# Windowed attention and a SiLU layer on one core: when the strided rows of batches 3 to 5 are loaded and transposed

## The chip, the core and the metric

The kernel runs on one core of a Trainium2 chip. A core has a matrix engine (TensorE, PE in the profile, with its weight loads shown apart as PEld), a vector engine (VectorE, DVE), a scalar engine (ScalarE, ACT), GpSimd (POOL) and SyncE (SP). Each engine has a queue of its own that runs in order; they meet through semaphores. POOL and SP here mostly start DMA transfers, which 16 DMA engines carry out. The metric is the device time of one run, in microseconds (us). Before the change it is 312.84 us, the median of three runs (312.16, 312.84 and 313.18).

## The reference

There are 8 batches, 8 heads, 576 positions and a head size of 64. Half of the heads look back over a window of 32 positions, the other half over every fourth position of the last 128. The attention's output goes through two dense layers with x * sigmoid(x) between them.

```python
scores = scale * np.matmul(q, k.transpose(0, 1, 3, 2))
mask_plain = (rel >= 0) & (rel < window)                                   # window = 32
mask_dil = (rel >= 0) & (rel < window * dilation) & (rel % dilation == 0)  # dilation = 4
masks = np.stack([mask_plain if h < H // 2 else mask_dil for h in range(H)], axis=0)
scores = np.where(masks[None], scores, -1e9)
attn = softmax(scores)                      # over the last axis
x = np.matmul(attn, v).transpose(0, 2, 1, 3).reshape(B * S, H * D)     # 4608 x 512
h = x @ w_in                                # 512 x 2048
out = ((h * sigmoid(h)) @ w_out)            # 2048 x 512, float32
```

## The kernel before

The dense layers are most of the work. For each batch `layer1` (L717) makes 16 blocks of 128 rows of h with 8 matmuls each, ScalarE applies the SiLU (L725), and `layer2` (L782) multiplies the result with w_out in tiles of 128 rows; VectorE copies a tile (L766) and SP stores it (L767) from one of five buffers, ob. One batch's two layers are a loop of steps, 0 to 47. Between them PE does the attention of the next batches in short groups.

The attention of a batch is split in two kinds, called z: z = 0 are the plain heads, z = 1 the strided heads, whose positions are regrouped by their remainder modulo 4. For each kind there are scores (L379 plain, L391 strided), exponentials on ScalarE (L560), a normalisation on VectorE (L576), a transpose of the probabilities and the product with v (L627, L691).

The scores need q and k with the head size on the partitions, so the rows that are loaded must be transposed. Up to batch 2 PE does this (L329). From batch 3 on it is done by DMA, in two steps:

- `load_rows(b)` runs on POOL. It loads q and k of batch b into one of two row buffers, nat (`natural[(b + 1) % 2]`). The plain rows are eight DMAs at L134, one for each head and each of k and q, with 128-byte pieces; the strided rows are four at L141, with 512-byte pieces. The argument zs sets which kind goes first.
- `cross(b, z)` runs on SP. For z = 0 it issues two transposing DMAs from nat to the buffer plain (L152, first k and then q), for z = 1 two to the buffer strided (L158, L159). plain and strided have two buffers each, for even and odd batches.

POOL also loads v (L177, L185, L190). SP also issues the stores and, from batch 3's strided heads on, the transposes of the probabilities pn (`turn_by_dma`, L600).

The order of all this is written out by hand. `plan_of(b)` holds, for the loop of batch b, lists of calls by step; `at(s, f, ...)` puts a call on step s, and calls of one step are issued in the order in which they were put there. In batch b's loop, steps 0 to 15 stand ahead of the 16 blocks of layer 1, and later steps ahead of each quarter of a tile of layer 2. No scheduler changes it: each engine's instructions stand in the order of these calls. An instruction waits on its own engine for what it reads, and for the readers of what it overwrites. So a DMA that SP issues waits at the head of SP's queue, and whatever stands behind it there waits as well. POOL's DMAs use eight semaphores in turn, so one waits until the eighth before it has landed.

What stands around the change, in the loops of batches 1 and 2:

- L852, in batch 0's loop: POOL loads the rows of batch 3, plain ones first.
- L870 to L872, in batch 1's loop: SP transposes batch 3's plain rows at step 2, its strided rows at step 20, and batch 4's plain rows at step 28.
- L878: POOL loads the rows of batch 4 at step 17, plain ones first.
- L893, in batch 2's loop: POOL loads the rows of batch 5 at step 0, plain ones first; later batches' rows are loaded strided ones first. They go into the buffer that held batch 3's.
- L895 and L896: at step 12, SP transposes the plain rows of batch b+3 and the strided rows of batch b+2.
- The strided scores of batch 3 are at step 11 of batch 2's loop, those of batch 4 at step 11 of batch 3's.

Of the kernel before, what the change touches and what calls it, by code (L numbers as in the profile page):

```python
# [29 lines left out]
def kernel(  # L30
# [764 lines left out]
    def transposes(at, b, z, step):  # L795
        for which in (1, 0):
            at(step, transpose, b, z, which, both)

    def later(at, b, z, steps, copies=(nc.vector.tensor_copy, nc.vector.tensor_copy)):

        for hi in (0, 1):
            if steps[hi] is not None:
                at(steps[hi], normal, b, z, hi)
        for hi in (0, 1):
            at(steps[2], turn, b, z, hi)
        for hi in (0, 1):
            at(steps[2], turned, b, z, hi, copies[hi])
        at(steps[3], values, b, z)
        at(steps[3], finish, b, z, copies)

    def plan_of(b):
        ev = {}

        def at(s, fn, *args):
            ev.setdefault(s, []).append((fn, args))

        def all_exps(b, z):
            for hi in (0, 1):
                at(16, exps, b, z, hi)

        if b == 0:

            at(-16, normal, 0, 1, 1)
            at(-15, shift_class, 0, dve, 1, 2)
            at(-14, normal, 0, 0, 1)
            at(-8, turn, 0, 1, 1)
            at(-8, turned, 0, 1, 1, act)
            at(-4, turn, 0, 0, 1)
            at(-4, turned, 0, 0, 1)
            at(-4, values0, 1, 1)  # L830
            at(-4, last_values, 0, 1, (1,))
            at(-4, finish0, 1, 1)
            at(-4, last_finish, 0, 1, 1)
            at(-2, values0, 0, 1)
            at(-2, last_values, 0, 0, (1,))
            at(-2, finish0, 0, 1, both)
            at(-2, last_finish, 0, 0, 1)
            at(-2, clear_short, 1, nc.vector)
            at(-2, load_v, 1)
            for c in (2, 3):  # L840
                at(-2, load_w_out, c)
            at(-2, load_qk, 2)
            transposes(at, 1, 1, 2)
            at(8, scores, 1, 1)
            for hi in (0, 1):
                at(8, shift, 1, 1, hi)
            for which in (1, 0):
                at(17, transpose, 1, 0, which, (dve, dve))
            at(20, normal, 1, 1, 0)
            at(20, scores, 1, 0)  # L850
            at(14, shift_v, 1, nc.sync.dma_start)
            at(17, load_rows, 3)  # L852
            at(17, load_v, 2)
            all_exps(1, 1)
            for hi in (0, 1):
                at(20, exps, 1, 0, hi)
            for n, z, hi in ((20, 1, 1), (26, 0, 0), (28, 0, 1)):
                at(n, normal, 1, z, hi)
            for n, z, copies in ((27, 1, (dve, dve)), (30, 0, both)):
                for hi in (0, 1):  # L860
                    at(n, turn, 1, z, hi)
                for hi in (0, 1):
                    at(n, turned, 1, z, hi, copies[hi])
                at(n + 1 + z, values, 1, z)
                at(n + 1 + z, finish, 1, z, both)
        elif b == 1:
            transposes(at, 2, 0, 2)
            transposes(at, 2, 1, 11)
            at(2, shift_v, 2, nc.sync.dma_start)
            at(2, cross, 3, 0)  # L870
            at(20, cross, 3, 1)
            at(28, cross, 4, 0)  # L872
            at(8, scores, 2, 0)
            for hi in (0, 1):
                at(8, shift, 2, 0, hi)
            at(17, nc.gpsimd.tensor_copy, latch, qTs[1][:, 1, S - 1 : S])
            at(17, load_v, 3)
            at(17, load_rows, 4)  # L878
            at(14, scores, 2, 1)
            all_exps(2, 0)  # L880
            all_exps(2, 1)
            for hi in (0, 1):
                at(19, normal, 2, 0, hi)
            at(21, scores, 3, 0)
            at(21, exps, 3, 0, 0)
            at(21, exps, 3, 0, 1)
            later(at, 2, 0, (None, None, 27, 28))
            later(at, 2, 1, (29, 31, 33, 34))
        else:
            if b + 2 < B:  # L890
                at(0, load_v, b + 2)
                if b + 3 < B:
                    at(0, load_rows, b + 3, (0, 1) if b == 2 else (1, 0))  # L893
                if b + 3 < B:
                    at(12, cross, b + 3, 0)  # L895
                at(12, cross, b + 2, 1)  # L896
            if b + 1 < B:
                at(1 if b == 2 else 0, shift_plain, b + 1, dve, 0, NM)
                at(12, shift_class, b + 1, dve, 0, 2)
                at(12, shift_over, b + 1, dve)  # L900
                if b == 2:
                    later(at, 3, 0, (0, 0, 4, 6))
                else:
                    at(6, values, b + 1, 0)
                    at(6, finish, b + 1, 0)
                at(11, scores, b + 1, 1)
                at(11, shift, b + 1, 1, 1)
                all_exps(b + 1, 1)
            if b + 2 < B:
                at(17, scores, b + 2, 0)  # L910
                for hi in (0, 1):
                    at(18, exps, b + 2, 0, hi)
            if b + 1 < B:
                for hi in (0, 1):
                    at(22 + hi, normal, b + 1, 1, hi)
                    at(22 + hi, turn_by_dma, b + 1, 1, hi)
                at(29, values, b + 1, 1)
                at(29, finish, b + 1, 1)
            if b + 2 < B:
                for hi in (0, 1):  # L920
                    at(27 + hi, normal, b + 2, 0, hi)
                    at(27 + hi, turn_by_dma, b + 2, 0, hi)

        def plan(s):
            for fn, args in ev.pop(s, ()):
                fn(*args)

        return plan
# [49 lines left out]
    for b in range(B):  # L978
        plan = plan_of(b)
        if b == 0:  # L980
            for x in range(NFF):
                plan(2 * x - NFF)
                plan(2 * x + 1 - NFF)
                layer1_part(2 * x % NFF, 2 * x // NFF, first[x] if x < 4 else None)
        else:
            for f in range(NFF):
                plan(f)
                layer1(b, f)
        if b == 0:
            layer2_first(plan)  # L990
        else:
            layer2(b, plan)
        for s in range(NFF, 3 * NFF):
            plan(s)
# [30 lines left out]
```

## Time and profile before

| | |
|---|---|
| median of three runs | 312.84 us (312.16 to 313.18) |
| the profiled execution, time | 313.66 us |
| the profiled execution, span | 311.9 us |
| PE busy | 298.2 us, 96% |
| VectorE busy | 180.1 us, 58% |
| ScalarE busy | 186.2 us, 60% |
| GpSimd busy | 91.5 us, 29% |
| DMA queue q0 (POOL's) | 18.88 MB |
| DMA queue q1 (SP's) | 19.60 MB |
| DMA queue q8 (instructions) | 35 transfers, 0.57 MB |

The span runs from the first to the last instruction; times in a timeline count from its start. In the groups and timelines a line has the engine, the line of the kernel, the operation, the tiles written and read, and how often; a bracket says how long the engine sat idle before it and what ended that, where "issue" means that the profile names nothing. SPq is SP's queue, in which issuing a DMA takes the time shown; the transfer itself goes on behind it. PEclk gives TensorE's granted clock in tenths for 40 equal slices of the span, 7.8 us each, and DMA how busy the DMA engines were.

The loops fall on these stretches: batch 1's from about 59 to 100 us, batch 2's from about 100 to 138 us, batch 3's from about 138 us on.

### The profile page before, as it was taken

How to read it: one execution, taken by the hardware profiler on the slowest of the kernel's cores; microseconds unless marked ns; L12 is line 12 of the kernel's file. 1: busy time of each engine (PE TensorE's matmuls, PEld its weight loads, DVE VectorE, ACT ScalarE, POOL GpSimd, SP SyncE). 2: the span in 40 equal slices, each digit the busy share in tenths (PEclk: the TensorE clock that was granted, in tenths of full speed). 3: DMA queues.
4: the chain of work that ended last, by engine and by line, in shares of the span. 5: the costliest groups of instructions: out<-in, count | busy, mean ns of one | idle time of the engine just before them, and what ended most of it. 6: DMA issues, size and time to landing. Idle time of an engine off the chain costs nothing.

```text
span 311.9 us, 10363 instructions
## 1 busy us (share of the span) xinstructions
PE 298.2 (96%) x4466; PEld 190.9 (61%) x4466; DVE 180.1 (58%) x372; ACT 186.2 (60%) x554; POOL 91.5 (29%) x139
## 2 busy tenths in 40 slices
PE   5889999999998979999999999999999999999995
PEld 2657755677455856467744676467744775468544
DVE  6896588627796725971687228871696245520011
ACT  1775658756992536955596357956694458336300
POOL 8535455920784442077104730040000000000000
PEclk9999999999999988999999999999999999999999
DMA  8999999997899999799967998399026100410021
GB/s 104 178 213 201 185 203 205 189 183 114 90 163 177 133 180 190 125 171 182 113 130 149 174 148 139 78 164 140 2 57 137 58 4 0 121 59 2 0 101 69
DMA packets 104878, 39.21 MB, mean 126 GB/s; under 512 B 79568, under 2 KB 100048, under 8 KB 104832
## 3 DMA queue, kind: packets, MB, share of 16 engines
q0 software_dynamic: 63104, 18.88, 60.0%
q1 hardware_dynamic: 41584, 19.60, 30.6%
q8 instruction: 35, 0.57, 0.8%
q14 instruction: 11, 0.09, 0.1%
q10 hardware_dynamic: 144, 0.07, 0.1%
HBM read 37.75 MB, written 9.44 MB: 151 GB/s over the span
## 4 chain that ended last, share of the span: by engine, by line
PE 82%; DMA 7%; DVE 5%; issue 3%; ACT 2%; POOL 1%; POOLq 0%; SPq 0%; ACTq 0%
PE h L717 36%; PE o L782 29%; PE o L756 5%; DMA w_in<-in_moe_w_in_dram 4%; PE h L737 4%; PE x L627 3%; DMA nat<-in_q_dram 2%; PE s L391 1%; PE s L379 1%; ACT pe L560 1%; DVE pn L576 1%; PE t L329 1%; DMA ptT<-pn 1%; DVE ms L512 1%; PE pt L585 1%
## 5 line engine op out<-in xcount | busy, mean ns | idle before, releaser
L725 ACT ACTIVATE gT<-h 128x576 f16<-128x576 f32 x112 | 72.9, 651 | 83.6 <-PE h L717 83.4
L717 PE MATMUL h<-xT,w_in 128*128 128x288 f16 x896 | 115.2, 289 | 0.0
L782 PE MATMUL o<-w_out,gT 128*128 128x512 f16 (+1 forms) x528 | 114.3, 373 | 0.1
L717 PEld LDWEIGHTS <-w_in 128*128 128x128 f16 x896 | 87.1, 99 | 24.3 <-DVE xT L704 0.3
L782 PEld LDWEIGHTS <-gT 128*128 128x128 f16 x528 | 50.6, 98 | 55.2 <-issue 0.3
L560 ACT ACTIVATE pe<-ms,nm 128x64 f32<-128x64 f32 x178 | 59.1, 334 | 4.2 <-DVE nm L528 4.2
L766 DVE COPY ob<-o 128x512 f32<-128x512 f32 (+1 forms) x34 | 23.1, 681 | 46.1 <-PE o L782 45.2
L512 DVE SCALAR_TENSOR_TENSOR ms<-s,mask 128x512 f32<-128x512 f32 x28 | 19.2, 686 | 40.3 <-PE s L391 27.5
L560 ACT ACTIVATION_READ_ACCUMULATOR pe<-ms,nm 128x1 f32 x178 | 33.5, 188 | 0.0
L704 DVE CAST xT<-x 128x512 f16<-128x512 f32 x26 | 16.8, 684 | 22.0 <-PE xs L691 22.0
L177 POOL DMA_DIRECT2D vw<-in_v_dram x16 | 10.0, 631 | 63.3 <-PE xs L691 57.3
L576 DVE TENSOR_TENSOR pn<-pe,r 128x640 f16<-128x640 f32 (+2 forms) x32 | 25.3, 792 | 1.1
L528 DVE TENSOR_REDUCE nm<-ms 128x10 f32<-128x640 f32 (+1 forms) x28 | 22.0, 787 | 1.0
L737 PE MATMUL h<-xT,w_in 128*128 128x256 f16 (+1 forms) x128 | 17.1, 286 | 1.8 <-issue 0.7
L134 POOL DMA_DIRECT2D nat<-in_q_dram x20 | 14.7, 757 | 8.0 <-DMA vw<-in_v_dram 4.3
L134 POOL DMA_DIRECT2D nat<-in_k_dram x20 | 15.1, 769 | 5.1 <-DMA nat<-in_q_dram 3.5
L737 PEld LDWEIGHTS <-w_in 128*128 128x128 f16 x128 | 12.0, 98 | 5.7 <-issue 1.8
L756 PE MATMUL o<-w_out,gT 128*128 128x512 f16 x64 | 15.0, 380 | 0.0
L744 ACT ACTIVATE gT<-h 128x512 f16<-128x512 f32 (+1 forms) x16 | 10.1, 651 | 6.5 <-PE h L737 6.3
L627 PEld LDWEIGHTS <-vw 64*64 64x64 f16 x896 | 8.6, 108 | 6.4 <-issue 6.2
L627 PE MATMUL x<-ptT,vw 64*64 64x32 f16 x896 | 10.4, 187 | 1.0 <-issue 0.9
L569 DVE TENSOR_REDUCE l<-pe 128x10 f32<-128x640 f32 (+2 forms) x12 | 9.6, 801 | 1.5 <-ACT pe L551 1.4
(101 smaller groups left out, 250.3 us busy)
## 6 DMA issues: line engine op xcount, KB each, us to landing
out_dram<-ob SPq DMA_DIRECT2D x35, 256.0 KB, 2.5
vw<-in_v_dram POOLq DMA_DIRECT2D x8, 288.0 KB, 6.6
vw<-in_v_dram POOLq DMA_DIRECT2D x16, 128.0 KB, 5.9
w_in<-in_moe_w_in_dram POOLq DMA_DIRECT2D x4, 512.0 KB, 12.6
w_out<-in_moe_w_out_dram POOLq DMA_DIRECT2D x4, 512.0 KB, 11.0
nat<-in_k_dram POOLq DMA_DIRECT2D x6, 256.0 KB, 7.1
nat<-in_q_dram POOLq DMA_DIRECT2D x6, 256.0 KB, 7.7
nat<-in_k_dram POOLq DMA_DIRECT2D x20, 72.0 KB, 6.8
```

The source lines that it names most:

```text
L134: nc.gpsimd.dma_start(out=f[:, 2 * (1 - which) + h // 2, 0 : ZR - 1, h % 2], in_=src[b, h].rearrange("(m p) d -> p m d", p=RT),)
L512: nc.vector.scalar_tensor_tensor(out=ms[:, 0:8].rearrange("p (n t) c -> p n (t c)", n=2), in0=s[hi].rearrange("p n t c -> p n (t c)"), sca ...
L528: nc.vector.tensor_reduce(out=nm[:, 0:w], in_=ms[:, 0:w], axis=AX.X, op=ALU.max, negate=True)
L560: nc.scalar.activation(pe[:, t, :], slot(t), AF.Exp, scale=1.0 if b else scale, bias=nm[:, t : t + 1], accum_out=l[:, t : t + 1],)
L576: nc.vector.tensor_tensor(pn[:, 0:w], a["pe", z, hi][:, 0:w], r[:, 0:w, None].broadcast_to([P, w, KB]), ALU.mult)
L627: nc.tensor.matmul(dst, w, p, start=True, stop=True)
L717: nc.tensor.matmul(h[:, half, 0:HS], w_in16[:, c, f * P : f * P + P], xT[:, c, half * HS : half * HS + HS], start=(c == 0), stop=(c == MC ...
L725: nc.scalar.activation(gT[:, f, s0 : s0 + S].rearrange("p (a c) -> p a c", a=2), h[:, :, 0:HS], AF.Silu)
L737: nc.tensor.matmul(h[:, i, 0 : c1 - c0], w_in16[:, c, (f + i) * P : (f + i + 1) * P], xT[:, c, c0:c1], start=(c == 0), stop=(c == MC - 1),)
L756: nc.tensor.matmul(o, gT[:, f, t * P : (t + 1) * P], w_out16[:, f, :], start=(f == 0), stop=(f == NFF - 1),)
L766: copy(ob, o)
L782: nc.tensor.matmul(o, gT[:, f, t * P : (t + 1) * P], w_out16[:, f, m0:m1], start=(f == 0), stop=(f == NFF - 1),)
```

## The change

Batch 3's strided transposes are issued at step 2 of batch 1's loop, right behind its plain ones, in place of step 20. Batch 4's strided transposes are issued at step 28 of batch 1's loop, right behind its plain ones, in place of step 12 of batch 2's loop, where they stood behind batch 5's plain transposes. From batch 5 on the strided transposes stay where they were. The rows of batch 5 are loaded strided ones first, as those of later batches are. No instruction is added or removed; PE, VectorE and ScalarE have the same order as before.

```diff
             transposes(at, 2, 1, 11)
             at(2, shift_v, 2, nc.sync.dma_start)
-            at(2, cross, 3, 0)
-            at(20, cross, 3, 1)
-            at(28, cross, 4, 0)
+            for z in (0, 1):
+                at(2, cross, 3, z)
+                at(28, cross, 4, z)
             at(8, scores, 2, 0)
...
                 if b + 3 < B:
-                    at(0, load_rows, b + 3, (0, 1) if b == 2 else (1, 0))
+                    at(0, load_rows, b + 3, (1, 0))
                 if b + 3 < B:
                     at(12, cross, b + 3, 0)
-                at(12, cross, b + 2, 1)
+                if b > 2:
+                    at(12, cross, b + 2, 1)
```

## The prediction

> **What bounds the kernel now.** Read first: the page's busy times and its slices. TensorE (PE) is busy 96% of 311.9 us, so only its idle time and its slow time can be won. Slices 15 and 16 (109 to 125 us) show a lowered clock, in the stretch where the DMA engines are busiest.
>
> ```profile
> span 311.9 us, 10363 instructions
> PE 298.2 (96%) x4466; PEld 190.9 (61%) x4466; DVE 180.1 (58%) x372; ACT 186.2 (60%) x554; POOL 91.5 (29%) x139
> ...
> PEclk9999999999999988999999999999999999999999
> DMA  8999999997899999799967998399026100410021
> ...
> q8 instruction: 35, 0.57, 0.8%
> ```
>
> Read second: the waits of PE. After the start-up (the first 25 us) three remain, and all end on "issue": nothing that the profile names.
>
> ```profile
> PE s L391 <- issue: 2.2, 1, 2.2
> PE x L627 <- issue: 0.9, 1, 0.9
> ...
> PE ss L391 <- issue: 0.3, 1, 0.3
> ```
>
> Read third: PE's timeline around the two long ones.
>
> ```profile
> 96.40 0.62 PE L627 MATMUL x<-ptT,vw 64*64 64x32 f16 x53
> 97.92 0.28 PE L627 MATMUL x<-ptT,vw 64*64 64x32 f16 x11 [0.90 <-issue]
> ...
> 107.14 5.07 PE L717 MATMUL h<-xT,w_in 128*128 128x288 f16 x40
> 112.15 0.58 PE L391 MATMUL s<-strided 64*32 64x64 f16 x52
> 114.98 0.27 PE L391 MATMUL s<-strided 64*32 64x64 f16 x12 [2.25 <-issue]
> ```
>
> Both break a group of equal matmuls in its middle, where no new operand is needed. Counted in order of start, PE resumes with its instructions 3,521, 4,033 and 5,057 (the third wait): 193 plus 13, 15 and 19 times 256. Queue q8 moved 0.57 MB in 35 transfers, 16 KB each: one block of 256 PE instructions (4466 matmuls and as many weight loads make 35 blocks). So PE waits for its own code. In the trace's packet records each fetch starts some time after PE has passed the block boundary before, and PE goes on 1.3 to 1.9 us after the fetch has ended:
> - first: PE passes the boundary at 90.10, the fetch runs 94.99 to 96.58, PE resumes at 97.92. Undisturbed, PE needs 6.73 us for that block, so a fetch that starts over 6.73-1.59-1.34=3.8 us late stalls it. It was 4.89.
> - middle: 97.92, fetch 102.93 to 104.55 (5.01 late); PE crosses at 106.74 without a stall. The limit is 8.82-1.62-1.34 (or 1.62)=5.6 to 5.9.
> - second: 106.75, fetch 112.41 to 113.36 (5.67 late), PE resumes at 114.98. The limit is 5.79-0.95-1.62=3.2.
>
> The second stall also lowers the clock: the next 40 matmuls of L717 take 6.75 us where the same 40 at 107.14 take 5.07, so 1.68 us more. The 0.90 us stall left the clock at 1.00.
>
> Read fourth: SP's and POOL's queues, for what fills the DMA engines in those delays.
>
> ```profile
> 72.07 3.93 SPq L152 DMA_TRANSPOSE plain<-nat  x2
> ...
> 85.99 4.78 SPq L158 DMA_TRANSPOSE strided<-nat  x1
> 90.87 1.19 SPq L159 DMA_TRANSPOSE strided<-nat  x1
> ...
> 93.42 12.12 SPq L152 DMA_TRANSPOSE plain<-nat  x2
> ...
> 121.71 3.53 SPq L158 DMA_TRANSPOSE strided<-nat  x1
> ```
>
> ```profile
> 105.74 2.20 POOL L134 DMA_DIRECT2D nat<-in_k_dram  x3 [3.52 <-DMA nat<-in_q_dram]
> ```
>
> Packet records by queue: from 88.8 to 94 us batch 3's strided transposes share the engines with POOL's loads of batch 4's rows, and from 100 to 111 us batch 4's plain transposes share them with POOL's next loads. The delays sort by that. POOL's 128-byte rows alone: 1.74, 2.35, 2.25 us (requests at 67.64, 114.98, 180.54). Transposes alone: 1.23, 1.86, 2.39, 1.64, 1.26. POOL's rows with stores: 1.20 (128-byte, 56.01) and 4.32 (512-byte, 60.86). POOL's rows of both sizes: 3.53. Transposes and POOL's rows together: 4.89, 5.01, 5.67, the three above.
>
> **The change part by part.** PE's, DVE's and ACT's orders are the same in both kernels; only SP and POOL are reordered, and no instruction is added.
>
> *Batch 3's strided transposes, from 85.99 to right behind 72.07+3.93=76.0.* Their rows were issued by POOL at 57.08 to 59.70, and the scores that read the buffer before (batch 1) are long done, so they start at once: 4.78+1.19=5.97 us of SP's queue, over by 82, before the store that follows (85.56). Moved past: that store (nothing) and, on the engines, the v loads of batch 3 (79.73 to 83.25), which are read at 103.65. What is won: at the request of 90.10 the transposes are gone; left are POOL's rows of batch 4 and two stores (issued from 92.15 now, then once copied, at 89.1 and 90.4). Nearest rows: 1.20 and 2.25, and 4.32 as the worst. I take 2.3, since the rows are still 128-byte ones then; under 3.8, so the first stall goes: -0.90. At 4.32 some 0.5 of it would stay. More than 0.90 cannot be won there.
>
> *Batch 4's strided transposes, from 121.71 to behind its plain ones.* They wait for strided rows that land at about 105.7 now (what POOL's wait of 3.52 ended on), a little earlier with the engines freer: I put the transposes' issue near 102. Queued behind on SP are two stores (copied at 95.2 and 100.9, issued 105.64 now). Late stores cost nothing: ob has 5 buffers and the next copy is at 126.71. Next comes L152 of batch 5, below. What it does to PE: at the middle request (96.8 now) plain transposes and POOL's 512-byte rows meet, as before: 5.01, under the limit, 0. At the second request transposes and POOL's rows meet too, strided ones in place of plain ones. Nearest rows 4.89, 5.01, 5.67, mean 5.19: the stall is shorter by 5.67-5.19=0.48. How long they run: plain and strided ones of a batch are 2,560 and 2,304 packets; before, plain ones went at 233 a us over 100 to 111 and at 400 over 108 to 110, so 4,864 take 12 to 21 us from 93 on, until 105 to 114. Ends of the delay: 3.53 if they are over at 105, and 5.67+1.6=7.3 if the fetch has to outlast them (plain ones ended at 111.1, the fetch started 1.3 later; an end near 111.7 and a request 1.0 earlier, since the first stall is gone, make 1.6 more). Near 2 us of idleness I keep the lowered clock (2.25 had it, 0.90 did not): 0.
>
> The row speaks of a wait that is bounded while both queues are full (4.89 to 5.67). [...] The rows don't settle it, since two of the three fetches started just after the transposes had ended.
>
> *Batch 5's strided rows first.* Four DMAs of POOL, 1.29+1.27=2.6 us, move ahead of eight plain ones. The plain rows, and so L152 of batch 5 (117.07 now, waiting for them), come about 2.6 us later: 119.7+4.54=124.2. Covered until SP has to issue the first transpose of pn at 128.84; for that L152 may slip by 7, since the 3.53+1.83 behind it are gone. Beyond that each us goes into the values matmuls at 133.99. Plain scores of batch 5 come at 156. The swap adds no wait: strided rows need batch 3's strided transposes read out, done by about 84.
>
> *Batch 3's layers and later* keep order and load; the 0.35 stall at 150 stays.
>
> **Sum.** -0.90 + 0 - 0.48 = -1.4. The profiled execution took 313.66 (span 311.9 and 1.8 around it), 0.8 above the median of 312.84; on it the sum gives 312.3, on the median 311.5.
>
> **Rivals.**
> *Both stalls and the slow clock go.* If batch 4's transposes are over at 105, or held up for their rows, when the second fetch is asked for, its delay is like 3.53 (stall 0.3) to 4.3 (1.1); the clock stays up. -0.90-(1.2 to 2.1)-1.68 = -3.8 to -4.7: 308.2 to 309.0. For it: transposes alone, or 128-byte rows alone, never gave over 2.4. Against it: POOL's rows do not thin out before 117.5.
> *Slower: one long stretch of transposes.* Plain and strided transposes of batch 4 now run back to back, to 114 at the slow rate, through both the middle and the second fetch. If the middle fetch is over 5.9 late it adds a stall of its own; at 6.9 that is +1.0, and the second fetch at 7.3 adds 1.6: with -0.90 this is +1.7, 314.5. It decides from a second delay of 6.6 (5.67+0.90) on. For it: 4.89 and 5.67 both ended about 1 us after the transposes did. Against it: 5.01 ended in the midst of them.
> *No change.* The first stall stays since two stores and 512-byte rows come forward into the gap (4.32), and the second is as it was: 312.3 to 313.2. [...]
>
> **How the numbers follow.** About 0.3% (0.9 us) is what a measurement here can tell from no change. Chances: forecast 0.36 (310.7 to 312.4: faster 0.27, same 0.09), both stalls gone 0.20, slower 0.29, no change 0.15 (same 0.13, slower 0.02). Faster 0.47, same 0.22, slower 0.31. The range leaves out the lower half of the second case and the tail of the third: 308.6 to 314.6; the forecast's own is 310.7 to 312.4.
>
> **What would show it.** Right: L158 on SP at about 76 and again near 102; no "issue" wait in the L627 group near 97; the wait in L391 near 111.5 at about 1.8 us, then L717's 40 matmuls still near 6.7. Wrong: a new wait within the L627 group at 106, an L391 wait over 2.5, an SP wait that runs past 128.8, or an L391 wait under 1 with the clock at 1.00.

## The result and the profile after

The changed kernel takes 311.09 us, the median of 20 runs (309.31 to 314.03); the kernel before takes 313.15 us beside it, the median of 20 (311.98 to 316.29). The ratio is 0.9925, with a 95% interval of 0.9901 to 0.995: the change makes the kernel faster by 2.1 us. Each kernel below is compared with the kernel before, measured beside it, and the ratios leave out executions that took over 1.5% longer than the fastest of their kernel (one, the first profile of A alone, took 383 us at a granted clock of 0.765), so they can differ a little from the quotient of two medians.

The profiled execution of the changed kernel took 311.39 us (span 309.5). From its page, the busy times and two rows of the slices:

```profile
span 309.5 us, 10365 instructions
PE 297.5 (96%) x4466; PEld 191.0 (62%) x4466; DVE 180.0 (58%) x372; ACT 186.3 (60%) x554; POOL 91.9 (30%) x139
...
PEclk9999999999999999999999999999999999999999
DMA  8999999998999999599988998498027000410022
```

In this execution the lowered clock of slices 15 and 16 is gone; the DMA engines are about as full as before. PE's waits that name nothing, after the start-up:

```profile
PE s L391 <- issue: 1.7, 1, 1.7
...
PE ss L391 <- issue: 0.6, 1, 0.6
```

PE's timeline of the same execution (start, duration, line, operation, tiles, count, and in brackets the idle time before it):

```profile
96.79 0.71 PE L627 MATMUL x<-ptT,vw 64*64 64x32 f16 x64
...
111.48 0.58 PE L391 MATMUL s<-strided 64*32 64x64 f16 x52
113.81 0.27 PE L391 MATMUL s<-strided 64*32 64x64 f16 x12 [1.75 <-issue]
...
114.13 5.07 PE L717 MATMUL h<-xT,w_in 128*128 128x288 f16 x40
```

The values group at 96.79 runs through with its 64 matmuls in one piece: the first stall (0.90) is gone. The scores still break after 52 matmuls, for 1.75 us in place of 2.25, and the 40 matmuls behind take 5.07 us in place of 6.75. SP's queue:

```profile
72.48 3.89 SPq L152 DMA_TRANSPOSE plain<-nat  x2
76.46 3.18 SPq L158 DMA_TRANSPOSE strided<-nat  x1
...
91.41 8.02 SPq L152 DMA_TRANSPOSE plain<-nat  x2
99.83 4.70 SPq L158 DMA_TRANSPOSE strided<-nat  x1
...
118.61 4.03 SPq L152 DMA_TRANSPOSE plain<-nat  x2
...
126.00 3.25 SPq L600 DMA_TRANSPOSE ptT<-pn  x2
```

Batch 3's strided transposes stand at 76.46, batch 4's at 99.83, batch 5's plain ones at 118.61, and the first transpose of the probabilities comes at 126.00 (128.84 before).

Between these two executions the time falls by 2.27 us (313.66 to 311.39; the spans differ by 2.34). The parts that can be named are: first stall -0.90, second -0.50, lowered clock -1.68, third stall +0.29 (0.35 to 0.64), start-up +0.52 (the 48 matmuls of L717 that begin batch 1's loop stand at 61.88 in place of 61.36). They add up to 2.27, but two executions are a small sample; what of it recurs, the experiments tell.

### The profile page after: what moved, and what is told of

Its sections match the earlier page's. It is cut to its first block, busy times and chain, and to the rows that moved or that the text cites. A ratio compares the mean times of both kernels' runs of the same rounds, so it can differ in the third digit from the quotient of the medians.

```text
span 309.5 us, 10365 instructions
## 1 busy us (share of the span) xinstructions
PE 297.5 (96%) x4466; PEld 191.0 (62%) x4466; DVE 180.0 (58%) x372; ACT 186.3 (60%) x554; POOL 91.9 (30%) x139
## 4 chain that ended last, share of the span: by engine, by line
PE 82%; DMA 7%; DVE 5%; ACT 2%; issue 2%; POOL 1%; POOLq 0%; SPq 0%; ACTq 0%
PE h L717 35%; PE o L782 29%; PE o L756 5%; DMA w_in<-in_moe_w_in_dram 4%; PE h L737 4%; PE x L627 3%; DMA nat<-in_q_dram 2%; PE s L391 1%; PE s L379 1%; ACT pe L560 1%; DVE pn L576 1%; PE t L329 1%; DMA ptT<-pn 1%; DVE ms L512 1%; PE pt L585 1%
## 5 line engine op out<-in xcount | busy, mean ns | idle before, releaser
L717 PE MATMUL h<-xT,w_in 128*128 128x288 f16 x896 | 113.5, 286 | 0.0
L717 PEld LDWEIGHTS <-w_in 128*128 128x128 f16 x896 | 86.4, 98 | 23.3 <-DVE xT L704 0.3
L704 DVE CAST xT<-x 128x512 f16<-128x512 f32 x26 | 16.8, 685 | 21.3 <-PE xs L691 21.3
L627 PEld LDWEIGHTS <-vw 64*64 64x64 f16 x896 | 8.5, 108 | 5.4 <-issue 5.2
```

The lines of the kernel that those rows point to most:

```text
L627: nc.tensor.matmul(dst, w, p, start=True, stop=True)
L717: nc.tensor.matmul(h[:, half, 0:HS], w_in16[:, c, f * P : f * P + P], xT[:, c, half * HS : half * HS + HS], start=(c == 0), stop=(c == MC ...
```

## The experiments

Three parts are named by a letter: A is batch 3's strided transposes at step 2, B is batch 4's at step 28 of batch 1's loop, C is batch 5's strided rows first. The theory: PE waits for blocks of its own code, and a fetch is late when both POOL's and SP's transfers fill the DMA engines at the request. The rivals: the stalls have another cause; or one of the parts does all, and others cost. "Late" is the time from PE's crossing of a block boundary to the start of the next fetch, from the trace's packet records. The request itself is not recorded and can be earlier than the crossing: in the kernel before, one fetch starts at 80.18, 1.9 us before PE starts the first instruction of its block, 3,009.

### A alone

```diff
-            at(20, cross, 3, 1)
+            at(2, cross, 3, 1)
```

> Only batch 3's strided transposes move (behind its plain ones); batch 4's and the load order stay as before. Theory F (PE waits for blocks of its own code, whose fetch is late while transposes and POOL's row loads share the DMA engines): the first stall near 97 us (0.90) goes, since its fetch starts 1 to 3 us late in place of 4.89; the second stays at 1.7 to 2.5 us in the L391 group. Time 0.9 to 1.4 us less, ratio 0.996 to 0.997. Rival O (the load order of batch 5's rows made the gain): both stalls as before, ratio 0.999 to 1.001. Rival D (the waits are for data, the strided operands above all): the L391 wait goes too, ratio 0.990.

310.76 us, the median of 6 runs, beside 313.11; ratio 0.9906 [0.9869, 0.9943]. The stalls come from a second measurement of the same kernel:

> The first experiment's kernel (only batch 3's strided transposes move) for an undisturbed profile. Theory F: no issue wait near 97; the second fetch starts under 4.8 us late, the L391 wait is under 1.7 us and leaves the clock at 1.00, since its time (0.991) asks for 2.8 us in all: 0.9 first stall, 0.7 the clock's share, 1.2 the second stall. Rival: the second stall is as before (2.2) and the lowered clock too, then the 2.8 us were chance and the ratio comes near 0.996.

310.15 us (6 runs) beside 312.97; ratio 0.9898 [0.9861, 0.9934]. PE's timeline of that second profile (310.17 us, span 308.4):

```profile
110.59 0.58 PE L391 MATMUL s<-strided 64*32 64x64 f16 x52
111.58 0.27 PE L391 MATMUL s<-strided 64*32 64x64 f16 x12 [0.40 <-issue]
...
111.89 5.07 PE L717 MATMUL h<-xT,w_in 128*128 128x288 f16 x40
129.14 0.19 PE L627 MATMUL x<-ptT,vw 64*64 64x32 f16 x1 [0.15 <-DMA ptT<-pn]
130.49 0.70 PE L627 MATMUL x<-ptT,vw 64*64 64x32 f16 x63 [1.16 <-DMA ptT<-pn]
```

A alone gains more than the 0.9 to 1.4 us that were expected, and at least as much as the whole change. (The ratio is what the rival D had, 0.990, but D's cause, waits for data, is excluded further down.) The first fetch is 2.48 us late, without a stall; the second is 3.86 late and stalls PE for 0.40, and the matmuls of L717 behind it keep their 5.07 us. A clears the second stall too, which the prediction had left to B: SP gets to batch 4's plain transposes at 92.04 (93.42 before) and has issued them in 7.05 us (12.12 before; a second profile of the kernel before has 95.15 and 8.36). Of the packets that start between the crossing at 105.19 and the second fetch, 14 belong to transposes; in the two profiles of the kernel before these are 1,391 and 897. The clock gains as well: in eleven of A's twelve executions the mean granted clock is 0.999 or 1.000, while 33 of 72 executions of the kernel before beside the experiments were below 0.997. A new wait of 1.3 us for ptT is the price. SP's queue shows it:

```profile
115.52 5.23 SPq L152 DMA_TRANSPOSE plain<-nat  x2
120.84 3.66 SPq L158 DMA_TRANSPOSE strided<-nat  x1
...
126.51 2.56 SPq L600 DMA_TRANSPOSE ptT<-pn  x2
```

Batch 5's plain and batch 4's strided transposes stand ahead of the probabilities' at 126.51, and PE reads what that L600 writes 2.6 us later, at 129.14.

### B alone

```diff
             at(28, cross, 4, 0)
+            at(28, cross, 4, 1)
...
-                at(12, cross, b + 2, 1)
+                if b > 2:
+                    at(12, cross, b + 2, 1)
```

> Only batch 4's strided transposes move (behind its plain ones); batch 3's stay at step 20, batch 5's plain rows are loaded first. Theory F: the first stall stays (0.6 to 1.1 us near 97); the second is between 1.0 and 2.5 us, since batch 4's transposes end later than in the changed kernel; ratio 0.996 to 1.002. Rival O: ratio 0.999 to 1.001 with both stalls exactly as before.

314.32 us (12 runs) beside 313.11; ratio 1.0005 [0.997, 1.004]. The profiled execution took 316.04 us, 1.7 over the median, so its stalls may be larger than usual. Its PE timeline and SP queue:

```profile
98.23 0.28 PE L627 MATMUL x<-ptT,vw 64*64 64x32 f16 x11 [1.48 <-issue]
...
116.55 0.35 PE L391 MATMUL s<-strided 64*32 64x64 f16 x12 [3.51 <-issue]
117.05 7.55 PE L717 MATMUL h<-xT,w_in 128*128 128x288 f16 x40
```

```profile
95.65 9.34 SPq L152 DMA_TRANSPOSE plain<-nat  x2
105.38 7.90 SPq L158 DMA_TRANSPOSE strided<-nat  x1
113.39 2.00 SPq L159 DMA_TRANSPOSE strided<-nat  x1
```

Without A the first stall stays (1.48), and the transposes of batch 4 run as one stretch from 95.65 to 115. The second fetch, asked for at 107.06, starts 6.91 us late, and PE sits idle for 3.51. Both stalls are longer than expected (0.6 to 1.1 and 1.0 to 2.5); the ratio is within 0.996 to 1.002. In this one profile that is the slower rival of the prediction, a second delay of up to 7.3 behind one long stretch. B by itself gains nothing.

### C alone

```diff
-                    at(0, load_rows, b + 3, (0, 1) if b == 2 else (1, 0))
+                    at(0, load_rows, b + 3, (1, 0))
```

> Only the load order moves: batch 5's strided rows ahead of its plain ones; all transposes stay. Theory F: transposes and POOL's rows still meet at both fetches, so delays of 4.5 to 5.7 us, first stall 0.5 to 1.0, second 1.5 to 2.5; ratio 0.998 to 1.002. Rival O: most of the measured gain, ratio 0.992 to 0.995.

315.69 us (12 runs) beside 313.11; ratio 1.0051 [1.0018, 1.0084]: slower by half a percent, where 0.998 to 1.002 was expected. SP's queue and PE's timeline:

```profile
121.38 4.48 SPq L152 DMA_TRANSPOSE plain<-nat  x2
125.95 3.01 SPq L158 DMA_TRANSPOSE strided<-nat  x1
...
131.33 2.56 SPq L600 DMA_TRANSPOSE ptT<-pn  x2
```

```profile
133.99 0.19 PE L627 MATMUL x<-ptT,vw 64*64 64x32 f16 x1 [2.32 <-DMA ptT<-pn]
135.31 1.07 PE L627 MATMUL x<-ptT,vw 64*64 64x32 f16 x63 [1.14 <-DMA ptT<-pn]
```

L152 of batch 5 moves from 117.07 to 121.38. Without B the strided transposes of batch 4 still stand behind it, so L600 slips from 128.84 to 131.33 and the values matmuls wait 3.5 us, which the expectation had left out; the two stalls, 0.19 and 1.31, are a little under its 0.5 to 1.0 and 1.5 to 2.5. This is the bound that the prediction named for C, with the cover (B's removal of 3.53+1.83 us there) taken away.

### A and B, without C

```diff
             transposes(at, 2, 1, 11)
             at(2, shift_v, 2, nc.sync.dma_start)
-            at(2, cross, 3, 0)
-            at(20, cross, 3, 1)
-            at(28, cross, 4, 0)
+            for z in (0, 1):
+                at(2, cross, 3, z)
+                at(28, cross, 4, z)
...
-                at(12, cross, b + 2, 1)
+                if b > 2:
+                    at(12, cross, b + 2, 1)
```

> Both groups of strided transposes move, the load order stays as before (plain rows of batch 5 first). Theory F: first stall gone, second 0.5 to 2 us (128-byte rows alone beside the end of the transposes, where the changed kernel had 512-byte ones), ratio 0.990 to 0.995, as the changed kernel or better. Rival O: ratio 0.996 or more.

311.59 us (12 runs) beside 313.11; ratio 0.9949 [0.9915, 0.9983], as expected. The interval overlaps the change's, so no cost of C is seen beside B. The second fetch is 4.77 late and the stall 1.3. The middle fetch is 6.49 late here, above the 5.6 to 5.9 that the prediction set as its limit, and PE waits 0.3 us for it.

### Are the waits fetches of code? The boundaries moved by 32 instructions

```diff
-    keep_busy(big.tile([P, 2, 512], F32, tag="big", name="busy")[:, 0], 4)
+    busy = big.tile([P, 2, 512], F32, tag="big", name="busy")[:, 0]
+    keep_busy(busy, 4)
+    keep_busy(busy, 16, P)
```

> The kernel before with 16 more small warm-up matmuls (32 more PE instructions) at the start, where PE waits for the first loads; nothing else moves. Theory F: the waits keep their count of PE instructions (3,521, 4,033) and so fall 32 instructions earlier in the program: the L391 group is broken after 36 of its 64 matmuls in place of 52, the L627 group after 37 in place of 53; time as before or up to 0.5 us more. Rival D: the groups are broken where they were, after 52 and 53.

This is the kernel before with 16 small warm-up matmuls more (32 PE instructions with their weight loads). 316.9 us (4 runs) beside 312.97; ratio 1.0113 [1.0061, 1.0166], where at most 0.5 us more was expected. PE's longest waits that name nothing, and its timeline:

```profile
PE ss L379 <- issue: 2.2, 1, 2.2
PE h L427 <- issue: 1.9, 1, 1.9
```

```profile
102.70 0.50 PE L627 MATMUL x<-ptT,vw 64*64 64x32 f16 x37
103.64 0.41 PE L627 MATMUL x<-ptT,vw 64*64 64x32 f16 x27 [0.44 <-issue]
...
117.99 0.45 PE L391 MATMUL s<-strided 64*32 64x64 f16 x36
118.70 0.39 PE L391 MATMUL s<-strided 64*32 64x64 f16 x28 [0.26 <-issue]
```

The L627 and L391 groups break after 37 and 36 matmuls in place of 53 and 52: 16 matmuls earlier, which is 32 instructions. Counted from the program's start the waits stand again at PE's instructions 3,521 and 4,033, so they belong to the count and not to the work. Both are 193 plus a multiple of 256, and 256 is the block that q8's 35 transfers of 16,384 bytes in the kernel before give for PE's 8,932 instructions. Why the time is longer is only in part known. In the start-up PE now waits 1.87 us in L427 (at 22.7 us) and 2.20 in L379 (at 51.4 us), at instructions 705 and 1,729, two boundaries that fall elsewhere than before. But the 16 matmuls themselves also put off PE's next work by 1.1 us (6.75 in place of 5.64), and the clock comes up at 26.3 us (16.4 and 21.3 in two profiles of the kernel before).

### Batch 5's rows later

Two kernels tried to take POOL's rows out of the way of the second fetch: the rows of batches 5 and 6 are loaded at step 12 in place of step 0 (behind a small copy by GpSimd that reads block 10 of gT, so that the loads wait for that step), and transposed at step 30. The first is the changed kernel with this edit, the second is A with it.

```diff
-                    at(0, load_rows, b + 3, (1, 0))
+                    n = 12 if b in (2, 3) else 0
+                    if n:
+                        at(n, nc.gpsimd.tensor_copy, latch, gT[:, 10, b % 2 * S : b % 2 * S + 1])
+                    at(n, load_rows, b + 3, (1, 0))
...
-                    at(12, cross, b + 3, 0)
+                    at(30 if b in (2, 3) else 12, cross, b + 3, 0)
```

> The changed kernel, with the rows of batches 5 and 6 loaded later: in the loops of batches 2 and 3, POOL first copies one value that the SiLU of block 10 writes (near 111 us), then loads; their plain transposes are issued at step 30. Theory F (PE waits for its own code; a fetch is late only where transfers of both queues, or of two row sizes, are in flight): at the second fetch (request near 106) only batch 4's v loads and the end of its transposes are left, so the fetch starts 1.5 to 3.5 us late, the L391 wait is 0 to 0.5 us, the third wait (L391, near 147) goes as well; 1.5 to 2.5 us less than the changed kernel, ratio to the kernel before 0.984 to 0.990. Rival D (the waits are for data): as the changed kernel, 0.992.

> Only batch 3's strided transposes move, and the rows of batches 5 and 6 are loaded later, as in the late-rows experiment. Theory F: no issue wait over 0.5 us in batches 1 to 3; ratio 0.983 to 0.989. Rival D: as batch 3's move alone, 0.991.

Both missed. The first took 311.78 us (12 runs) beside 312.97, ratio 0.9952 [0.9919, 0.9986]; the second 311.88 us (12 runs), ratio 0.9948 [0.9919, 0.9978], where A alone has 0.9898. In the first the second stall is 2.68 us: batch 4's strided transposes, which B put there, stand at the request together with the load of batch 4's v (1,295 and 2,665 packets start in the delay), and the fetch is 5.31 late. This profiled execution took 314.51 us, 2.7 over the median. In the second the stall is 0.50, no less than with A alone. The second kernel keeps a wait of 1.0 us for ptT as well, now near 202 us. And both have a wait that no other kernel has, in batch 4, where batch 6's rows now meet a fetch (4.38 and 4.14 late). From PE's timeline of the second:

```profile
183.62 0.27 PE L391 MATMUL ss<-strided 64*32 64x64 f16 x13 [0.62 <-issue]
```

Here the transfers that were put off met another tight block.

### A, with batch 4's strided transposes behind the probabilities'

To keep A's gain and lose its wait of 1.3 us, batch 4's strided transposes are issued at step 30 of batch 2's loop, behind L600's; the second kernel has C as well.

```diff
-            at(20, cross, 3, 1)
+            at(2, cross, 3, 1)
...
-                at(12, cross, b + 2, 1)
+                at(30 if b == 2 else 12, cross, b + 2, 1)
```

> Batch 3's strided transposes early, and batch 4's strided ones issued behind the transposes of the probabilities in batch 2's loop, step 30 in place of step 12. With batch 3's move alone the values matmuls at 129 to 131 us waited 0.15 and 1.16 us for ptT, because L158 of batch 4 (3.7 us of SP's queue) stood ahead of L600. Theory (SP's queue is too full there): with those 4 to 5 us taken out of its way, the ptT wait goes (-1.3 us), the second stall stays at about 0.4 us, and the time is 0.985 to 0.988 of before, near 309.0. Rival (the delays only move on): the strided transposes, now near 130 to 136 us, meet the fetch of the third block (asked for at 141 in the changed kernel), the third stall grows from 0.6 by 1 us or more, and the time stays at 0.990 of before, 310 or more.

> As the run before, with batch 5's strided rows loaded ahead of its plain ones as in the change. Theory: the order of the rows costs only by making SP late for the transposes of the probabilities; here SP has nothing else left between, L152 of batch 5 comes 2 to 3 us later (118 to 119 in place of 115.5) and ends before 127, and the time is that of the run before within 0.3%. Rival (the order costs in itself, by what it does to the fetches): 0.5% slower than the run before, as the swap alone was against the kernel before.

The first took 315.57 us (9 runs) beside 312.85: ratio 1.0104 [1.0068, 1.014], slower than before, where 0.985 to 0.988 was expected. What was meant to go did go: the second fetch is 2.34 late and its stall is gone, as is the wait for ptT near 130. The loss is one batch later. PE's timeline, POOL's and SP's of the first kernel:

```profile
166.21 0.19 PE L627 MATMUL x<-ptT,vw 64*64 64x32 f16 x1 [2.79 <-DMA ptT<-pn]
167.53 0.70 PE L627 MATMUL x<-ptT,vw 64*64 64x32 f16 x63 [1.13 <-DMA ptT<-pn]
...
168.31 7.90 PE L782 MATMUL o<-w_out,gT 128*128 128x512 f16 x28
```

```profile
144.19 1.28 POOL L141 DMA_DIRECT2D nat<-in_k_dram  x2 [10.29 <-DMA strided<-nat]
```

```profile
132.88 4.21 SPq L158 DMA_TRANSPOSE strided<-nat  x1
...
153.89 4.01 SPq L152 DMA_TRANSPOSE plain<-nat  x2
...
163.54 2.57 SPq L600 DMA_TRANSPOSE ptT<-pn  x2
```

The strided transposes at 132.88 read the buffer that batch 6's rows go into. POOL waits 10.29 us for it and loads them at 144.19 (135.53 in the changed kernel); L152 of batch 6 waits for the rows until 153.89 (147.60), and L600 of batch 4 behind it on SP comes at 163.54 (159.72). PE waits 3.9 us, and the 28 matmuls behind take 7.90 us where the changed kernel's take 6.22: the lowered clock again. Neither the theory nor its rival had this; the third stall, the rival's place, is 0.78.

With C as well: 315.22 us (12 runs), ratio 1.0076 [1.005, 1.0103], within 0.3% of the kernel without it. L152 of batch 5 comes 4.9 us later (109.67 to 114.53), and SP's next instruction starts at 122.88 and 122.85. So C has a price only where SP is short of time.

### Both kernels once more

> The kernel before, unchanged, for a second profile. The theory says that the stalls are a matter of how late a fetch starts, which varies from run to run: the second stall in L391 between 1.7 and 2.6 us, and the clock behind it lowered in one of two executions; L717's 40 matmuls behind it take 6.7 us with the clock lowered and 5.1 without. Rival: the lowered clock follows always from the stall, and the 40 matmuls take 6.7 us again whenever the stall is over 2 us.

> The changed kernel, unchanged, for a second profile. Expected: no stall in L627 near 97, the second one in L391 between 1.3 and 2.0 us, L717's 40 matmuls behind it at 5.1 us. Rival: the second stall is over 2 us and the 40 matmuls take 6.7 us, so that the clock in the first profile was chance.

One execution each: the kernel before took 311.81 us, the changed one 312.2. PE's timelines, the kernel before first:

```profile
99.08 0.28 PE L627 MATMUL x<-ptT,vw 64*64 64x32 f16 x11 [0.24 <-issue]
...
114.45 0.27 PE L391 MATMUL s<-strided 64*32 64x64 f16 x12 [0.57 <-issue]
114.77 5.08 PE L717 MATMUL h<-xT,w_in 128*128 128x288 f16 x40
```

```profile
113.34 0.27 PE L391 MATMUL s<-strided 64*32 64x64 f16 x12 [1.81 <-issue]
113.66 6.75 PE L717 MATMUL h<-xT,w_in 128*128 128x288 f16 x40
```

Both expectations missed in part: the kernel before stalled less than the 1.7 to 2.6 us, and the changed one, with its stall inside 1.3 to 2.0, had the lowered clock. So the kernel before can stall far less than in its first profile (0.24 and 0.57; fetches 4.27 and 4.17 late), and the changed kernel can have the lowered clock (1.81 us of idleness and 6.75 us behind it). The stalls of all profiles together, in us, with how late the second fetch was:

| batch 3's strided transposes | batch 4's strided transposes | first stall | second fetch late | second stall |
|---|---|---|---|---|
| step 20 | step 12 of batch 2's loop (before, twice; C alone) | 0.90, 0.24, 0.19 | 5.67, 4.17, 5.07 | 2.25, 0.57, 1.31 |
| step 20 | step 28 (B alone) | 1.48 | 6.91 | 3.51 |
| step 2 | step 28 (changed, twice; A and B; late rows) | 0, 0, 0, 0 | 4.75, 5.29, 4.77, 5.31 | 1.75, 1.81, 1.31, 2.68 |
| step 2 | step 12 of batch 2's loop (A; A with late rows) | 0, 0 | 3.86, 3.64 | 0.40, 0.50 |
| step 2 | step 30 of batch 2's loop (without and with C) | 0, 0 | 2.34, 3.71 | 0, 0.26 |

The first stall is there in all four profiles without A, and in the one with the boundaries moved (0.44), and in none of the eight with it. On the second stall the profiles are few, and of kernels that differ: the mean of the first row is 1.38, the fourth row has 0.40 and 0.50, 0.9 us less, though the least of the first row, 0.57, is close. With B beside A the third row without the late rows has a mean of 1.62, 1.2 us above A alone (0.40).

## Why the prediction was right

In total: 311.5 us was predicted, 311.09 measured, within the forecast's own range. Its difference was -1.4 us, the measured one -2.1, with -1.6 to -3.1 by the interval; so the sum falls a little short of it. That the total came out is in part luck: A by itself brought 2.9 and 3.2 us where its step had 0.90, and B, whose step had a gain of 0.48, seems to give back about 1 us beside A.

*What bounds.* Right. PE waits for blocks of its own code: the breaks moved with the count of instructions (after 37 and 36 matmuls in place of 53 and 52, with 32 instructions put in front).

*A, the move to 76.0.* Right: 76.46, at once, and no harm ahead of the store. The first fetch was to be 2.3 us late; it was 1.74 and 2.04 in the changed kernel's two profiles, and 2.0 to 3.8 in the others with A, 3.78 without a stall, which is as far as the step's limit of 3.8 goes. The step's -0.90 is right for the profile and high as a mean: the first stall was 0.90, 0.24, 0.19 and 1.48 in the four profiles without A, 0.7 on average. The step's omission is larger: A also brings batch 4's plain transposes forward and makes them shorter, and so takes about 0.9 us off the second stall and, it seems, most of the lowered clock. The prediction had the middle and the second fetch meet the same traffic as before.

*B, near 102.* The place is right (99.83). The second fetch came 4.75 and 5.29 late where the step had 5.19, and the stall was 1.75 and 1.81 where it had 1.77. The cause of that lateness was only half right. The last packet of the transposes ended at 107.6 and 108.4, near the early end of the step's 105 to 114, and the fetch started 3.2 and 2.4 us after that. Of the packets that start in the delay of the first profile 199 are transposing ones (773 in the second), 2,281 are of 128 bytes and 496 of 512. Nor are the 128-byte ones rows of q and k, as the prediction read them: from 105.2 on there are 2,304 of them and then a gap, as many as in the late-rows kernel, where POOL loads no rows until 113; they are the plain part of batch 4's v, which POOL issues ahead of batch 5's rows. With A alone this load begins later still, at 107.06, and the fetch is 3.86 late, so what makes B's delay about 1 us longer stays open.

The sign of the step is probably wrong. Its 2.25 was one profile, and the largest of three second stalls without A and B (0.57 and 1.31 the others). So the agreement on the stall is luck in part. With A, B costs about 1.2 us in the second stall, and what it gives back is the wait of 1.3 us for ptT. B alone had the second fetch 6.91 late, as the *slower* rival has it; in the full change A takes the edge off that.

*The clock, kept at 0.* Wrong for the first two profiles (-1.68), and the second two have it the other way round. The prediction put the bound between 0.90 and 2.25 us of idleness; there is no such bound: 1.75 us left the clock up, 1.81 lowered it, and 2.20 in the kernel with the boundaries moved left it up. What the clock adds to the 2.1 us isn't settled. Over 72 executions of the kernel before, 22 had a mean granted clock of 0.993 to 0.995, as the first profile has it (0.995, with one stretch of 3.41 us at a clock of 0.50), and took 1.2 us longer (313.9) than those at 0.998 or more (312.7). Of 21 executions of the changed kernel one had it. That would be worth (22/72 - 1/21) x 1.2 = 0.3 us, an estimate. But 11 of the 72 and 8 of the 21 had a lower mean still, 0.976 to 0.989, so that 33 of 72 and 9 of 21 are nearly the same share; these eight took no longer than the changed kernel's others (311.2 and 311.4 on average). The profile of A and B has a mean of 0.989 from the start-up alone, at 10.4 to 17.3 us.

*The middle fetch at 0.* Right for the change (3.88 and 3.77 late), although B with A can bring it to 6.49 and a wait of 0.3, and the limit of 5.6 to 5.9 was a little low: 6.28, in the first late-rows kernel, cost 0.09.

*C.* Right in both its halves: L152 of batch 5 at 118.61 (119.7 predicted; 4.3 us later and not 2.6 with C alone), no cost here, and 3.5 us of waiting at the values matmuls where the cover is taken away.

*The third stall.* 0.35 and 0.03 in the two profiles of the kernel before became 0.64 and 0.41, 0.3 more on average; it was to stay.

*The rivals.* "Both stalls and the slow clock go" didn't happen with the change; it is about what A does alone (0.40, clock 1.00). "No change" didn't come either: the first stall is 0 in both profiles of the changed kernel. That the stalls have a cause other than code is excluded by the breaks that moved.

With 0.7 for the first stall, nothing sure for the second, at most 0.3 for the clock and -0.3 for the third, the means explain at most 0.7 of the 2.1 us. The rest is open. Too few profiles of each kernel were made to put it in a place: PE's instruction 2,241, at the end of the start-up, alone came between 60.6 and 62.9 us in them. A candidate that was not tested by itself is the wait for ptT in the kernel before, where SP issues L600 2.8 us later (128.84) than in the changed one (126.00): one profile of before showed 0.2 us of it, C alone 3.5.

The kernel with A alone is ahead of the change in both of its measurements (0.9906 and 0.9898 against 0.9925, and 0.9949 for A and B), though the intervals overlap; it is one line of the diff.

## What to carry to other kernels

Where an engine's group of equal instructions breaks in the middle and the profile names nothing, count its instructions: here the breaks stood at instructions 3,521, 4,033 and 5,057, each 193 plus a multiple of 256, and there PE waited for a late fetch of code. How late it is (2.34 to 6.91 us for the second fetch) went here with the traffic on the DMA engines after the request, so try moving traffic and not operands. Move one transfer at a time and look at what stands behind it in its queue and who needs the buffer next: of the three parts here one made the gain, one seems to have given part of it back, and a better-looking place for the second made the kernel slower one batch later. Before a stall's size is put into a sum, see it in a second execution: these stalls varied by a factor of four.

## What the runs showed of the hardware

- A fetch of one and the same block started 4.17 or 5.67 us late in two executions of the kernel before, and 2.34 to 6.91 over the kernels of the table. It is not transposes alone that hold it up: in the changed kernel's first profile 4.75 us came with loads by POOL in pieces of 128 and 512 bytes, and 199 transposing packets among some 3,000.
- The clock was lowered after idle times of no fixed length: 1.31, 1.75 and 2.20 us left it up, 1.81, 2.25, 2.68 and 3.51 us lowered it, for an extra 1.3 to 2.5 us in the next 40 matmuls (6.36 to 7.55 in place of 5.07). The clock records of the first profile of the kernel before have it at 0.50 for 3.41 us, from 115.40 us on, and nowhere else between the start-up and the end of the program. That is 98.99 us, 29.0 times the 3.41, after the clock came up at 16.41; in the 3.41 us ahead of it PE ran for 34% of the time. In the changed kernel's first profile the clock came up at 19.36 and was lowered only at 309.49, behind the last matmul (it ends at 306.3), 85.0 times the 3.41 later. Counted off in steps of 3.41 us from 19.36, the step in which PE ran least until 306 us has 49%, around the idle time of 1.75 us, and the clock stayed up. With B alone the lowered stretch lasts 6.83 us (mean clock 0.988). What decides whether the clock is lowered, these profiles don't show.
- Putting 16 small matmuls in front, which moves the code boundaries by 32 instructions, cost 1.1% of the time; in its one profile, waits of 4.1 us at two boundaries in the start-up and 1.1 us for the matmuls themselves stand against smaller stalls later on.
